# Two copies on GpSimd that feed batch 3's transpose, placed on two sides of a hold

## The chip, the cores and the metric

The kernel runs on one core of one Trainium2 chip. A core has five engines with queues of their own: TensorE (PE in the profile; PEld are its weight loads), VectorE (DVE), ScalarE (ACT), GpSimd (POOL) and SyncE (SP), which here only issues transfers. An engine works through its own queue in order and waits on semaphores for the others. The metric is the time of one execution on the device, in microseconds; the median of ten runs of the kernel before is 205.81.

## The reference

For each of 8 batches and 8 heads, with x (512 x 64) and state (32 x 64):

```python
scores = scale * np.matmul(x, state.transpose(0, 1, 3, 2))
a = softmax(scores);   xread = np.matmul(a, state)
a2 = softmax(scale * np.matmul(state, x.transpose(0, 1, 3, 2)))
sread = np.matmul(a2, x)
attn = np.concatenate([xread, sread], axis=2)       # 512 + 32 rows a batch
h = attn_as_rows @ w_in                             # (4352 x 512) @ (512 x 2048)
out = (0.5 * h * (1 + erf(h / sqrt(2)))) @ w_out    # (2048 x 512)
```

(`softmax` stands for the shifted exponentials over their sum that the reference spells out, and `attn_as_rows` for its transpose and reshape.)

## The kernel before, in words

**Work of one batch.** The 512 rows of a batch lie as 128 partitions by SJ = 4 groups. The steps are:

- `load_x(b)` brings x of one batch into `xb` as bf16, by a transfer issued from GpSimd's queue (512 KB).
- `rearr(b)` makes two GpSimd copies, one for each half t of the heads, from `xb` into `x4`, in the order that the transpose wants (L224, 128x1024 each). There are two tiles `x4`, used by even and odd batches in turn.
- `xtr_dma(b)` issues a transposing transfer from `x4` to `xT` on SyncE's queue (L277). It reads all of `x4`, so it needs both copies.
- `scores(b, half)` multiplies `xT` with the state (L330), and ScalarE takes the exponentials into `e` (L337).
- `norm(b, half)` is three VectorE instructions: sums (L350), reciprocals (L352) and the scaling of `e` into `a` (L353). "Batch 2's scaling" is L353 of batch 2, twice, for two halves.
- `atr_dma(b)` issues a transposing transfer from `a` to `AT`, on SyncE (L373).
- `p_mm` makes P, the product of state and w_in, on TensorE (L421); copies on ScalarE and VectorE empty its banks (L432, L433; for batch 2's first half L1094 and L1096).
- `mm1` (called `M`) multiplies P with `AT` (L484), and ScalarE takes the GELU into `g` (L491). M(16b) to M(16b+15) are batch b's.
- The second matrix product goes from `g` to the output. For batch 0 it is plain (`mm2`, `mm2_m`, called `U`); for the others it is Strassen's form with seven products, `X(b, "1")` to `X(b, "7")` (L581), whose sums of `g` (`g_sum`, L575) and of w_out (`w_sums`, L547) are made on VectorE, and a few sums on GpSimd (L600, L636).
- `sread`, `srt` and the later `SR` and `R` make the 32 extra rows of each batch; `rearr_ones(b)` makes the copy `xo` of x that `sread` needs (L234, GpSimd for b of 2 and more).

**Order.** Nothing plans the order: the schedule is manual, and each engine runs its instructions in the order in which the program calls them. The calls are written out by hand up to line 1103 and by a loop over batches 2 to 7, with eight slots p each, after that. Batch b + 1's attention is prepared between batch b's products: in the loop, `scores(3, ...)` stand at b = 2, p = 1, behind M(32, 33), pmat(2, 2) and X(1, "4").

**Banks.** The PSUM pool `ps_f` has four buffers in turn, used by `mm1`, `scores`, some `p_mm` tiles, `state_prep`, `sread` and `srt`; the pool `ps_o` has four banks o0 to o3, one buffer each.

**Holds.** `hold` is one column that GpSimd copies from a tile that is to be waited for. It puts a wait into GpSimd's queue: what stands behind it starts after that tile is written. `hold_for(b, m)` (L902) waits for a slice of `g`; line 1079 waits for `a` of batch 2, that is for both halves of batch 2's scaling.

The lines around the change:

```python
    norm(2, 0)
    norm(2, 1)
    atr_dma(2)
    nc.gpsimd.tensor_copy(out=hold, in_=atts[2].a[:, 0, 64:65])
    begin(3)
    rearr(3)
    xtr_dma(3)
```

`begin(3)` only names batch 3's tiles and takes `xT`'s buffer; it gives no instruction. GpSimd's queue before the hold ends with load_x(3) and load_st(3, B), called some lines earlier.

Of the kernel before, what the change touches and what calls it, by code (L numbers as in the profile page):

```python
# [17 lines left out]
def kernel(  # L18
# [136 lines left out]
    def state_prep(b0, b1, pool=ps_f, tag="f"):  # L155
        n = b1 - b0
        ps = pool.tile([128, n, HC, NS], BF16, name="st_ps", tag=tag)
        for b in range(b0, b1):
            nc.tensor.transpose(
                ps[:, b - b0, :, :].rearrange("p c n -> p (c n)"),  # L160
                st_bf[:, b, :, :].rearrange("q t d -> q (t d)"),
                ident,
            )
        for t in range(2):
            nc.vector.tensor_copy(
                out=sbd[64 * t:64 * t + 64, b0:b1, :, 32 * t:32 * t + 32].rearrange(
                    "d b c n -> d (b c) n"
                ),
                in_=ps[64 * t:64 * t + 64, :, :, :].rearrange("d b c n -> d (b c) n"),
            )  # L170
# [34 lines left out]
    def begin(b):  # L205
        A = Att()
        atts[b] = A
        A.x4 = x4s[b % 2]
        A.xo = xos[b % 2]
        if b > 0:  # L210
            A.xT = att.tile([128, SJ, HC, 128], BF16, name="xT", tag="xT")
# [5 lines left out]

    def rearr(b):  # L220
        A = atts[b]
        src = xbs[b].rearrange("p (t c) (j d) -> p t c j d", t=2, d=D)
        for t in range(2):
            nc.gpsimd.tensor_copy(  # L224
                out=A.x4[:, :, :, 64 * t:64 * t + 64].rearrange("p j c d -> p c j d"),
                in_=src[:, t],
            )
# [47 lines left out]
    def xtr_dma(b):  # L275
        A = atts[b]
        nc.sync.dma_start_transpose(  # L277
            out=A.xT.rearrange("p j c n -> p (j c) n"),
            in_=A.x4.rearrange("p j c n -> p (j c n)"),
        )  # L280
# [198 lines left out]
    def mm1(b, m):  # L479
        if m == 0:  # L480
            gs[b] = gpool.tile([128, MC, S], BF16, name="g", tag="g")
        hp = ps_f.tile([128, S], FP32, name="hp", tag="f")
        for t in range(2):
            nc.tensor.matmul(  # L484
                hp,
                lhsT=Ps[b][:, t, m * 128:(m + 1) * 128],
                rhs=atts[b].AT[:, :, t, :],
                start=(t == 0),
                stop=(t == 1),
            )  # L490
        nc.scalar.activation(out=gs[b][:, m, :], in_=hp, func=AF.Gelu)  # L491
# [48 lines left out]
    def w_add(name, x, y, op):  # L540
        if name == "3":
            pair = persist.tile([128, 2, MH, NH], BF16, name="ws_34", tag="mix0")
            w_sum["3"], w_sum["4"] = pair[:, 0], pair[:, 1]
        elif name != "4":
            tag = {"6": "mix1", "1": "mix2", "7": "mix3"}[name]
            w_sum[name] = persist.tile([128, MH, NH], BF16, name=f"ws_{name}", tag=tag)
        nc.vector.tensor_tensor(out=w_sum[name], in0=x, in1=y, op=op)  # L547

    def w_sums(i):
        (b11, b12), (b21, b22) = w_q  # L550
        w_add(*(
            ("3", b12, b22, ALU.subtract),
            ("4", b21, b11, ALU.subtract),
            ("6", b11, b12, ALU.add),
            ("1", b11, b22, ALU.add),
            ("7", b21, b22, ALU.add),
        )[i])
# [347 lines left out]
    def M(*ms):  # L905
        for m in ms:
            mm1(m // MC, m % MC)
# [147 lines left out]
    w_sums(0)  # L1055
    begin(2)
    rearr(2)
    xtr_dma(2)
    hold_for(0, 15)
# [4 lines left out]
    U(13)  # L1064
    state_prep(2, 3, ps_o, "o3")
    w_sums(1)
    M(18, 19)
    M(20, 21)
    U(14)
# [7 lines left out]
    norm(2, 1)  # L1077
    atr_dma(2)
    nc.gpsimd.tensor_copy(out=hold, in_=atts[2].a[:, 0, 64:65])
    begin(3)  # L1080
    rearr(3)
    xtr_dma(3)
    M(24, 25)
    M(26, 27)
# [20 lines left out]
    for b in range(2, B):  # L1105
        nb = b + 1
        for p in range(8):
# [40 lines left out]
            if p == 0 and nb + 1 < B:  # L1148
                begin(nb + 1)
                rearr(nb + 1)  # L1150
# [36 lines left out]
    b = B - 1  # L1187
# [40 lines left out]
```

## Time and profile before

| what | value |
| --- | --- |
| median of 10 runs | 205.81 us (205.42 to 207.54) |
| profiled execution | 206.21 us |
| its span | 204.4 us |
| TensorE busy | 197.4 us (97%) |
| VectorE busy | 156.9 us (77%) |
| ScalarE busy | 135.3 us (66%) |
| GpSimd busy | 69.8 us (34%) |
| granted TensorE clock | 1.0 throughout |
| L224, 12 copies on GpSimd | 13.6 us, mean 1162 ns |
| L234, 12 copies on GpSimd | 15.7 us, mean 1340 ns |
| L353, 14 scalings on VectorE | 10.4 us, mean 742 ns |

The profile is of one execution. Its span runs from the first instruction of the program to the end of the last; the execution's time is 1.8 us longer. A line of the timeline gives start and length in us, engine, line of the kernel, operation, tiles (written <- read), shapes, how many instructions were joined, and in brackets how long the engine stood idle before it and what ended that. In the chain, each row is the work, wait or transfer that the end of the kernel hung on at that time. All times inside the span are in us from its start.

### The profile page before, as it was taken

What the parts mean: (1) busy time and instruction counts of PE and PEld (TensorE: products, weight loads), DVE (VectorE), ACT (ScalarE), POOL (GpSimd) and SP (SyncE); (2) the same over time, 40 slices, a digit from 0 to 9 for tenths busy, and PEclk for the clock granted to TensorE, in tenths of its full rate; (3) what the DMA queues carried; (4) which work ended last, traced back from release to release, by engine and by line L of the source; (5) the groups of instructions that cost most, each with busy time, mean ns of one, the idle gap of its engine ahead of it and who ended that gap; (6) DMA issues with size and microseconds to landing.
All of it is one profiled execution on the core that took longest, in us unless ns stands there. A gap on an engine that the chain in (4) does not pass through costs nothing.

```text
span 204.4 us, 4911 instructions
## 1 busy us (share of the span) xinstructions
PE 197.4 (97%) x2039; PEld 133.4 (65%) x2039; DVE 156.9 (77%) x254; ACT 135.3 (66%) x240; POOL 69.8 (34%) x77
## 2 busy tenths in 40 slices
PE   7799999999799999999999999999999999999994
PEld 2443544465476667766875777667776787878893
DVE  2853777879888888977897787678778988895883
ACT  3685677689596669675966788587847666864120
POOL 8893303306544558271625702340220002200000
PEclk9999999999999999999999999999999999999999
DMA  6999997994866688736483504660106001040125
GB/s 196 186 179 200 205 199 119 136 256 88 125 90 147 201 108 100 163 138 70 59 174 102 133 0 102 71 196 0 51 3 205 3 0 55 0 157 0 51 100 162
DMA packets 40566, 23.16 MB, mean 113 GB/s; under 512 B 21856, under 2 KB 39136, under 8 KB 40544
## 3 DMA queue, kind: packets, MB, share of 16 engines
q0 software_dynamic: 13984, 8.10, 29.6%
q1 hardware_dynamic: 25872, 14.36, 27.9%
q10 hardware_dynamic: 688, 0.39, 0.6%
q8 instruction: 16, 0.26, 0.5%
q14 instruction: 6, 0.05, 0.1%
HBM read 17.30 MB, written 8.91 MB: 128 GB/s over the span
## 4 chain that ended last, share of the span: by engine, by line
PE 87%; DMA 6%; DVE 2%; ACT 2%; POOL 1%; issue 0%; SPq 0%; POOLq 0%
PE xp L581 38%; PE hp L484 24%; PE op L526 5%; PE p_ps L421 4%; PE sp L788 3%; PE rp L854 3%; DMA xT<-x 3%; DMA x0f<-in_x_dram 3%; PE xp L693 2%; PE pt L330 1%; PE sr L384 1%; PE op L510 1%; PE hp L1005 1%; POOL x L224 1%; DVE a L353 1%; PE warm_ps L149 1%
## 5 line engine op out<-in xcount | busy, mean ns | idle before, releaser
L491 ACT ACTIVATE g<-hp 128x512 bf16<-128x512 f32 x124 | 67.1, 605 | 26.5 <-PE hp L484 19.9
L484 PE MATMUL hp<-AT,P 128*128 128x512 bf16 x248 | 63.1, 379 | 0.1
L581 PEld LDWEIGHTS <-gsum 128*128 128x128 bf16 x528 | 51.0, 98 | 12.1 <-issue 2.1
L575 DVE TENSOR_TENSOR gsum<-g 128x2048 bf16<-128x2048 bf16 x35 | 45.7, 1321 | 0.9 <-ACT g L491 0.9
L484 PEld LDWEIGHTS <-P 128*128 128x128 bf16 x248 | 22.8, 98 | 20.7 <-issue 2.9
L581 PE MATMUL xp<-ws,gsum 128*128 128x256 bf16 x304 | 36.3, 273 | 0.0
L581 PE MATMUL xp<-ws,g 128*128 128x256 bf16 x224 | 26.7, 273 | 0.0
L581 PE MATMUL xp<-w_out_bf,gsum 128*128 128x256 bf16 x224 | 26.6, 273 | 0.0
L581 PEld LDWEIGHTS <-g 128*128 128x128 bf16 x224 | 21.8, 98 | 4.8 <-issue 0.2
L433 DVE CAST P<-p_ps 128x512 bf16<-128x512 f32 x29 | 18.8, 684 | 3.5 <-PE p_ps L421 3.4
L636 POOL TENSOR_TENSOR u<-s,oh 128x512 f32<-128x512 f32 x6 | 7.8, 1304 | 39.5 <-ACT oh L633 39.5
L432 ACT CAST P<-p_ps 128x512 bf16<-128x512 f32 x29 | 15.8, 599 | 6.1 <-PE p_ps L421 5.8
L224 POOL COPY x<-xb 128x1024 bf16<-128x1024 bf16 x12 | 13.6, 1162 | 14.7 <-DMA xb<-in_x_dram 14.7
L234 POOL COPY xo<-xb 128x1024 bf16<-128x1024 bf16 x12 | 15.7, 1340 | 4.3 <-PE sr L384 4.3
L600 POOL TENSOR_TENSOR v<-q,oh 128x512 f32<-128x512 f32 x6 | 8.3, 1390 | 23.5 <-ACT oh L638 20.8
L526 PE MATMUL op<-w_out_bf,g 128*128 128x512 bf16 x48 | 11.8, 380 | 0.0
L353 DVE TENSOR_TENSOR a<-e,ics 128x512 bf16<-128x512 bf16 x14 | 10.4, 742 | 0.5
L421 PE MATMUL p_ps<-w_in_bf,sbd 64*32 64x512 bf16 x248 | 10.4, 382 | 0.0
L350 DVE TENSOR_REDUCE cs<-e 128x16 f32<-128x512 bf16 x14 | 9.5, 677 | 0.6 <-ACT e L337 0.5
L411 DVE COPY XSR<-srT 128x128 bf16<-128x128 bf16 x8 | 5.7, 759 | 5.4 <-PE srT L408 5.4
L337 ACT ACT_TABLE_LOAD x7 | 9.0, 1283 | 0.1
L491 ACT ACT_TABLE_LOAD x7 | 9.0, 1283 | 0.1
(129 smaller groups left out, 227.6 us busy)
## 6 DMA issues: line engine op xcount, KB each, us to landing
out_dram<-oh SPq DMA_DIRECT2D x15, 256.0 KB, 2.4
xb<-in_x_dram POOLq DMA_DIRECT2D x7, 512.0 KB, 6.8
out_dram<-oh SPq DMA_DIRECT2D x6, 512.0 KB, 2.8
w_in_bf<-in_moe_w_in_dram POOLq DMA_DIRECT2D x6, 256.0 KB, 9.8
out_dram<-osb SPq DMA_DIRECT2D x5, 256.0 KB, 5.8
w_out_bf<-in_moe_w_out_dram POOLq DMA_DIRECT2D x4, 256.0 KB, 6.9
w_out_bf<-in_moe_w_out_dram POOLq DMA_DIRECT2D x2, 512.0 KB, 12.4
x0f<-in_x_dram SPq DMA_DIRECT2D x3, 256.0 KB, 3.9
```

The costliest lines, as they stand in the source:

```text
L224: nc.gpsimd.tensor_copy(out=A.x4[:, :, :, 64 * t:64 * t + 64].rearrange("p j c d -> p c j d"), in_=src[:, t],)
L234: eng.tensor_copy(out=A.xo[:, :, :, 2 + 64 * t:66 + 64 * t].rearrange("p j c d -> p c j d"), in_=src[:, t],)
L350: nc.vector.reduce_sum(out=cs, in_=e4, axis=AX.X)
L353: nc.vector.tensor_tensor(out=A.a[:, :, hs].rearrange("p g (c n) -> p g c n", n=NS), in0=e4, in1=ics[:, :, :].to_broadcast((128, G, 2, NS) ...
L421: nc.tensor.matmul(ps[t][32 * c:32 * c + 32, :], lhsT=sbd[64 * t:64 * t + 64, b, c, 32 * t:32 * t + 32], rhs=w_in_bf[64 * t:64 * t + 64, c ...
L432: nc.scalar.copy(out=dst[:, 0, :], in_=ps[0])
L433: nc.vector.tensor_copy(out=dst[:, 1, :], in_=ps[1])
L484: nc.tensor.matmul(hp, lhsT=Ps[b][:, t, m * 128:(m + 1) * 128], rhs=atts[b].AT[:, :, t, :], start=(t == 0), stop=(t == 1),)
L491: nc.scalar.activation(out=gs[b][:, m, :], in_=hp, func=AF.Gelu)
L526: nc.tensor.matmul(ops[b, j], lhsT=gs[b][:, m, j * 128:(j + 1) * 128], rhs=w_out_bf[:, m, :], start=(m == 0), stop=(m == MC - 1),)
L575: nc.vector.tensor_tensor(out=t, in0=g_q(b, h0, k0), in1=g_q(b, h1, k1), op=op)
L581: nc.tensor.matmul(ps[:, j - js[0], :], lhsT=lhs[:, m, 128 * j:128 * j + 128], rhs=rhs[:, m, :], start=(first and j == js[0] and m == 0), ...
```

## The change

`rearr` gets a second argument, the halves t that it copies. The call for batch 3 is parted in two. The copy of half 0 is called earlier, behind `state_prep(2, 3, ...)` and `w_sums(1)`; on GpSimd's queue that is right behind load_st(3, B) and ahead of the hold, so it waits for x of batch 3 alone. The copy of half 1 stays behind the hold. The transposing transfer is called at the same place as before. The queues of TensorE, VectorE, ScalarE and SyncE have the same instructions in the same order as before; on GpSimd's queue one copy and the hold have changed places.

```diff
-    def rearr(b):
+    def rearr(b, ts=(0, 1)):
         A = atts[b]
         src = xbs[b].rearrange("p (t c) (j d) -> p t c j d", t=2, d=D)
-        for t in range(2):
+        for t in ts:
             nc.gpsimd.tensor_copy(
                 out=A.x4[:, :, :, 64 * t:64 * t + 64].rearrange("p j c d -> p c j d"),
                 in_=src[:, t],
...
     state_prep(2, 3, ps_o, "o3")
     w_sums(1)
+    begin(3)
+    rearr(3, (0,))
     M(18, 19)
...
     nc.gpsimd.tensor_copy(out=hold, in_=atts[2].a[:, 0, 64:65])
-    begin(3)
-    rearr(3)
+    rearr(3, (1,))
     xtr_dma(3)
```

## The prediction

> **What bounds the kernel now.** I read the page first, then the chain that ended last in order of time, then TensorE's gaps, then the four engines and the transfers around the one gap that the change can touch.
>
> The page says that TensorE sets the time, and that its clock is never cut:
>
> ```profile
> PE 197.4 (97%) x2039; PEld 133.4 (65%) x2039; DVE 156.9 (77%) x254; ACT 135.3 (66%) x240; POOL 69.8 (34%) x77
> PEclk9999999999999999999999999999999999999999
> ```
>
> The chain in order of time is TensorE almost from 12 us on, with one large detour, which runs through the lines of the change:
>
> ```profile
> 46.76 0.27 DVE ics L352
> 47.05 0.70 DVE a L353
> 47.80 0.08 issue
> 47.88 0.19 POOL hold L1079
> 48.06 0.74 POOL x L224
> 48.81 0.17 issue
> 48.98 1.04 POOL x L224
> 50.04 5.78 DMA xT<-x
> 55.82 0.05 issue
> 55.87 0.64 PE pt L330 x16
> ```
>
> Batch 2's scaling (L353) releases the hold, GpSimd makes its two copies one after the other, SyncE starts the transposing transfer, and TensorE waits for its landing before batch 3's scores. TensorE's timeline gives the size of that wait; behind it no gap above 0.06 us comes until the end, so what is taken from it reaches the end of the kernel unless something new waits:
>
> ```profile
> 55.87 0.64 PE L330 MATMUL pt<-sbd,xT 128*128 128x64 bf16 x16 [1.36 <-DMA xT<-x]
> ```
>
> So at most 1.36 us can be gained: TensorE ended X(1,"4") at 54.50.
>
> **The first copy, moved.** x(3) was issued at 36.45 and landed 10.1 us later, at 46.58 (query of the tile xb in that window). GpSimd stands idle from 38.27, so the copy starts at about 46.63 (batch 4's started 0.05 us after its landing) and takes 1.04 (L224's usual duration): to 47.67. No instruction and no transfer is added; one copy of 1.04 us goes from behind the hold to before it. What then stands behind the copy's wait for x on GpSimd's queue is the hold, the second copy, the hold on batch 1's g, the two copies into xo, the hold on batch 2's g and load_x(4); all of them stood behind the later hold before, so none loses.
>
> **What the copy meets on VectorE.** From 46.63 to 47.67 VectorE does the sums (46.05 to 46.73), the reciprocal (to 47.01), and from 47.05 the scaling, which reads e and ics, both in SBUF. Batch 3's scaling shows the same meeting:
>
> ```profile
> 59.08 1.04 POOL L224 COPY x<-xb 128x1024 bf16<-128x1024 bf16 x1 [4.80 <-DMA xb<-in_x_dram]
> 59.62 1.03 DVE L353 TENSOR_TENSOR a<-e,ics 128x512 bf16<-128x512 bf16 x1
> ```
>
> There it took 1.03 instead of 0.69 and ended 0.54 after GpSimd's copy; at 83.18 and 104.46 it ended 0.55 after the GpSimd instruction that it met. So here it ends at 47.67 + 0.54 = 48.21 instead of 47.74: 0.47 late. The Trainium skill, "SBUF — State Buffer", section "Who interferes with whom", speaks against the change more strongly: a VectorE instruction with two SBUF inputs contends with a GpSimd instruction that reads SBUF, and the one that comes second is fully blocked. Fully blocked, it would run its whole 0.69 after 47.67, to 48.36: 0.62 late. By the rule the gain below is 0.75 us, by the rows 0.90. I take the rows, since three agree.
>
> **What is late next.** Behind the scaling on VectorE come three casts (L1094) that empty p_ps. The weight loads and VectorE's first cast, by their timelines:
>
> ```profile
> 47.66 0.68 DVE L1094 CAST P<-p_ps 128x512 bf16<-128x512 f32 x1
> 48.40 0.53 PEld L484 LDWEIGHTS <-P 128*128 128x128 bf16 x3 [0.26 <-issue]
> ```
>
> The cast ends at 48.34 and the weights of M(30) load at 48.40: M(30) takes the bank that this cast empties, and waits for it now already. So 0.47 on the scaling is 0.47 on M(30) and on all of TensorE up to the scores: X(1,"4") ends at 54.97 instead of 54.50. That is the price, and it is paid before the wait, where it only shortens it. The rest is covered: the second cast frees X(1,"6")'s bank at 49.41, against 50.01; x(3)'s neighbour AT(2) is issued at 48.28 and with its 3.1 lands at 51.37, against M(32)'s start at 51.75; the state copies (L165) end near 51.2, needed at 52.7. ScalarE runs with TensorE; its table load for the exponentials ends at 55.31, before the first scores at 55.38.
>
> **The second copy and the transfer.** The hold runs 0.14 after the scaling (48.35), the copy starts 0.11 after the hold (48.46) and ends at 49.50; before it ended at 50.02. SyncE must first issue AT(2), which occupies it for 1.25 from 48.28, to 49.53. So xT(3) is issued at 49.53 instead of 50.04: 0.51 earlier, not the 1.04 of the copy.
>
> Its 5.78 to landing is the longest of six (4.3 to 5.8, median 4.7). The windows of the transfers say why: 51.00 to 53.75 moves at full rate, then 1.25 us almost nothing, and in that stretch lies one packet of another queue:
>
> ```profile
> 51.00:53.75 2.75, 2.75 (x28) 1.72 (x26) 2.20 (x3) 1.95 (x5) 2.58 (x4) 1.00 1.06 193
> 53.75:55.00 1.25, 0.75 (x7) 0.43 (x5) 1.21 (x2) 1.09 (x1) 0.52 (x1) 1.00 0.07 8
> q8 instruction: 1, 0.02, 2.4%
> ```
>
> (the first columns are time and length, the last two DMA share and GB/s). All but one DMA engine were done at 53.8; one was held about 0.95 us by a 16 KB instruction fetch at 53.42, and then shared with x(4)'s first packets. After the change the transfer's data lies about 0.5 earlier, from near 50.7 (AT(2)'s must go first) to 53.4; the fetch comes with TensorE's progress, so near 53.9. Without the collision it lands at 49.53 + 4.26 (batch 4's) + 0.25 for AT(2)'s tail = 54.0; with the full 5.78 at 55.31. I take the first, since the cause of the long one has moved apart; even a landing at 54.9 would cost nothing, as TensorE comes at 54.97.
>
> **The sum.** Scores start at 54.97 instead of 55.87: 0.90 us. Of the 1.36 us of stall all goes, and 0.47 comes back as VectorE's delay. With the long transfer it is 55.87 - 55.36 = 0.51. The profiled execution took 206.21 (span 204.4 and 1.8 around it), so it becomes 205.3. The median of the runs is 205.81, 0.40 below the profiled one; nothing shown says where those 0.40 lie. If they are a shorter stall (as the transfer's spread allows), the gain is 0.50 and the median 205.3; if they lie elsewhere, 0.90 and 204.9. I take the middle: 205.05.
>
> **Behind the scores.** VectorE is 0.47 late while TensorE is 0.90 early, and it works without a break from 53.36 to 60.65. It reaches batch 3's scaling at 60.09 instead of 59.62, there meets both copies of x(4) instead of one (59.05 to 61.07) and ends at 61.6 instead of 60.65. It then had 1.11 of idle time before q (L642) and 0.70 before L608; both take up most of it. The next TensorE step that waits for VectorE is the p_ps of P(3), at 68.77, which needs L644 (ended 68.12): it now comes at 67.87, and I have L644 at about 67.6. The margin shrinks from 0.65 to 0.3, and I count nothing.
>
> **Rivals.**
> *Gain cut (0.2 to 0.5 us; 205.3 to 205.6).* x(3) lands 0.4 later than in this trace, so the scaling comes first and blocks the copy, as the second copy at 60.05 was (it ended 0.91 after the scaling): then 48.65, the second copy about 49.8, the transfer 0.25 earlier, in front of the same fetch. Or the fetch still holds it. For: one landing time only is known. Against: 0.4 is much for a load issued 10 us ahead.
> *No move (205.8).* x(3) lands after the scaling, over 1.1 us later than traced; then the hold costs nothing now, and the order of the two is no matter.
> *Slower (206.7): the debt on VectorE.* Place: L644 before P(3)'s p_ps. Price: a 128x2048 sum of g that meets GpSimd took up to 2.60 (at 99.81) against the 1.51 of the sum at 62.37 that stands here, 1.09 more; and the scaling of batch 3's second half, late enough to meet v (L600), would lose about what the first half does, 0.95. It decides when L644 ends after 68.72: then TensorE starts P(3) later than the 68.77 of now. I have it at 67.6; with both it is 69.65, and TensorE starts 0.93 later than before, 206.7, as nothing behind gives that back. For: VectorE has no idle time from 53 to 61, and the change moves GpSimd's work against it. Against: the idle 0.70 before L608, and u and v on GpSimd follow TensorE. One of the two alone ends near 205.8 or 205.9.
> *More than counted (204.5).* The scaling isn't held at all and the whole 1.36 goes.
>
> **How the numbers follow.** 0.3% is 0.62 us, about what can be told from no change. Stall gone, debt paid: 0.55 (204.8 to 205.4; three quarters of it beyond 0.62). Gain cut: 0.22. No move: 0.06. Slower: 0.12, a little of it within 0.3%. More: 0.05. So faster 0.42 + 0.05 = 0.47; within 0.13 + 0.22 + 0.06 + 0.02 = 0.43; slower 0.10. The range from 204.5 to 206.1 leaves out most of the slower case and the lower half of the best, under 2 in 10; the likeliest case alone is 204.8 to 205.4.
>
> **What would show it.** In the changed profile: one L224 copy at about 46.6 and one at 48.5; L353 of batch 2 at 1.1 to 1.2 instead of 0.69; M(30)'s weights at about 48.9; xT(3) issued at 49.5, landed before 55; no gap, or under 0.1, before L330 at about 55.0. It is wrong if x(3) lands after 47; if the gap before L330 stays with a landing of over 5 us; or if TensorE shows a new gap behind VectorE between 58 and 70, or anywhere after.

## The result, and the profile after

The changed kernel takes 204.66 us (median of 14 runs, 204.03 to 205.75), beside 205.98 for the kernel before in the same comparison. The ratio is 0.9932, 95% interval 0.991 to 0.9953, or 1.4 us less; the two medians are 1.3 us apart. A ratio, here and below, leaves out executions that took over 1.5% more than the fastest of their kernel. The profiled execution took 205.59 us, with a span of 203.8.

In the timeline of TensorE in the changed kernel (start and length in us, what it does, in brackets its idle time before), the wait ahead of batch 3's scores is gone:

```profile
54.72 0.71 PE L581 MATMUL xp<-ws,g 128*128 128x256 bf16 x5
55.26 0.63 PE L330 MATMUL pt<-sbd,xT 128*128 128x64 bf16 x16
```

The second line is the one that bore 1.36 us of idle time before; it bears none. The execution is only 0.6 us shorter in span than the one before because it has a wait of its own, 12 us earlier, at batch 2's scores:

```profile
42.87 0.64 PE L330 MATMUL pt<-sbd,xT 128*128 128x64 bf16 x16 [0.98 <-DMA xT<-x]
```

That is batch 2's transposing transfer, issued at 34.35 and landed after 8.5 us, against 4.8 in the profile before. Nothing ahead of it was changed, and two further profiles of the changed kernel (below) show 0.27 and none. TensorE waited there in three of the eight profiles of the changed kernel and its variants (the one with x asked for earlier left aside), and in none of the four with both copies behind the hold; whether that is chance isn't shown. From the start of batch 2's scores to that of batch 3's is 14.23 us before (41.64 to 55.87) and 12.39 after (42.87 to 55.26). That stretch holds everything that the change touches up to the scores, and I use it below to compare profiles, since it leaves out what happens earlier.

GpSimd's and VectorE's timelines of the same execution, around the copies:

```profile
47.06 1.04 POOL L224 COPY x<-xb 128x1024 bf16<-128x1024 bf16 x1 [8.71 <-DMA xb<-in_x_dram]
48.80 0.19 POOL L1081 COPY hold<-a 128x1 bf16<-128x1 bf16 x1 [0.69 <-DVE a L353]
48.92 1.04 POOL L224 COPY x<-xb 128x1024 bf16<-128x1024 bf16 x1
...
47.69 0.25 DVE L352 RECIPROCAL ics<-cs 128x16 f32<-128x16 f32 x1
47.98 0.69 DVE L353 TENSOR_TENSOR a<-e,ics 128x512 bf16<-128x512 bf16 x1
```

The copies are parted as written. But the second scaling took 0.69, not the 1.1 to 1.2 forecast: TensorE's wait at 42.87 had made VectorE late, x had landed 0.96 ahead of the scaling, and the copy was nearly done when it began (it ended at 48.10, 0.12 after the scaling's start). So either this execution was lucky, or the forecast debt isn't ordinary.

### The profile page after: what moved, and what is told of

It is laid out like the page before. It is cut to its first block, busy times and chain, and to the rows that moved or that the text cites. A ratio compares the mean times of both kernels' runs of the same rounds, so it can differ in the third digit from the quotient of the medians.

```text
span 203.8 us, 4911 instructions
## 1 busy us (share of the span) xinstructions
PE 197.6 (97%) x2039; PEld 133.5 (65%) x2039; DVE 156.9 (77%) x254; ACT 135.3 (66%) x240; POOL 68.9 (34%) x77
## 4 chain that ended last, share of the span: by engine, by line
PE 80%; DMA 15%; POOL 1%; DVE 1%; issue 0%; ACT 0%
PE xp L581 41%; PE hp L484 22%; DMA w_out_bf<-in_moe_w_out_dram 11%; DMA xT<-x 4%; PE p_ps L421 3%; PE sp L788 3%; PE rp L854 3%; PE xp L693 2%; PE warm_ps L149 2%; PE pt L330 1%; PE sr L384 1%; PE xT_ps L256 1%; POOL a L315 1%; PE op L510 0%; DVE xT L260 0%; POOL xb L117 0%
## 5 line engine op out<-in xcount | busy, mean ns | idle before, releaser
L636 POOL TENSOR_TENSOR u<-s,oh 128x512 f32<-128x512 f32 x6 | 8.8, 1466 | 40.8 <-ACT oh L633 40.8
L224 POOL COPY x<-xb 128x1024 bf16<-128x1024 bf16 x12 | 12.6, 1079 | 23.5 <-DMA xb<-in_x_dram 23.5
L234 POOL COPY xo<-xb 128x1024 bf16<-128x1024 bf16 x12 | 14.7, 1257 | 4.4 <-PE sr L384 4.4
L421 PE MATMUL p_ps<-w_in_bf,sbd 64*32 64x512 bf16 x248 | 10.3, 382 | 0.0
```

The source lines that it names most:

```text
L224: nc.gpsimd.tensor_copy(out=A.x4[:, :, :, 64 * t:64 * t + 64].rearrange("p j c d -> p c j d"), in_=src[:, t],)
L234: eng.tensor_copy(out=A.xo[:, :, :, 2 + 64 * t:66 + 64 * t].rearrange("p j c d -> p c j d"), in_=src[:, t],)
L421: nc.tensor.matmul(ps[t][32 * c:32 * c + 32, :], lhsT=sbd[64 * t:64 * t + 64, b, c, 32 * t:32 * t + 32], rhs=w_in_bf[64 * t:64 * t + 64, c ...
```

## The experiments

Theory: the gain is the early issue of batch 3's transposing transfer, which clears TensorE's instruction fetch and then lands before TensorE comes; the early copy costs what it takes from batch 2's scaling. Rivals: the meeting is never paid for; the gain comes from emptier queues and not from the transfer; the wait before was an accident of one execution.

**Both kernels again.** No edit.

> The changed kernel once more. The recorded theory (the first copy meets batch 2's second scaling, which loses about 0.47 us and passes it to M(30); the wait before batch 3's scores goes): L353 of batch 2's second half 1.1 to 1.2 us, TensorE at batch 3's scores 0.4 to 0.5 later than it would be without the copy, no gap there, about 0.9 us faster than before. Rival, that the copy and the scaling miss each other and nothing is paid (as in the profile of the changed kernel at hand, in which batch 2's scores had waited 0.99 us for a late transfer, so that VectorE came late): L353 at 0.69 and 1.2 to 1.4 us faster.

> The changed kernel once more, for its profile: where x lands between batch 2's two scalings, and what the second one loses. If the recorded 0.47 is ordinary, its L353 takes 1.0 to 1.2 and M(30) waits 0.4 to 0.6; if not, 0.69 and at most 0.15. In both no gap before batch 3's scores.

> The kernel before once more, for its profile. If the wait of 1.36 us at batch 3's scores is its ordinary state, there is one of 0.9 to 1.4 again, with a fetch near the transfer's end and a landing of over 5.3 us. If it was an accident of that execution, the wait is 0.1 to 0.4 and the landing 4.3 to 4.8.

The changed kernel: 204.66 us (22 runs) against 205.75, ratio 0.9939 (0.9919 to 0.9958). In its two profiles the second scaling takes 0.69 again. The third profile shows why, VectorE first, then GpSimd and SyncE:

```profile
44.33 0.69 DVE L353 TENSOR_TENSOR a<-e,ics 128x512 bf16<-128x512 bf16 x1
...
45.94 0.69 DVE L353 TENSOR_TENSOR a<-e,ics 128x512 bf16<-128x512 bf16 x1
...
44.56 1.36 POOL L224 COPY x<-xb 128x1024 bf16<-128x1024 bf16 x1 [7.23 <-DMA xb<-in_x_dram]
...
46.70 1.25 SPq L373 DMA_TRANSPOSE AT<-a  x1
48.03 1.95 SPq L277 DMA_TRANSPOSE xT<-x  x1
```

x landed at 44.51. The copy met the first scaling, which had already begun; so it was the copy that waited (1.36 instead of 1.04), and it was over at 45.92, just before the second scaling. TensorE's timeline has no wait of more than 0.1 us from 40 to 72. The stretch from scores to scores is 12.70.

The kernel before, in its second profile:

```profile
55.22 0.64 PE L330 MATMUL pt<-sbd,xT 128*128 128x64 bf16 x16 [1.23 <-DMA xT<-x]
```

Issue to landing was 5.65, the stretch 14.09. So the wait is no accident of one execution. This one took 205.55 us, 0.66 less than the first, with only 0.13 less of wait: what lay between the first profile and the median wasn't the stall. Most of it lies at the start: TensorE begins batch 1's scores at 21.74 in the first profile and at 21.23 in this one. But x landed at 44.55 here, 1.99 us ahead of the second scaling, where the first profile had 0.47.

**The meeting forced.** The first copy behind a hold on the sums of batch 2's second half, so that it starts right before the scaling:

```diff
         nc.vector.reduce_sum(out=cs, in_=e4, axis=AX.X)
+        A.cs = cs
...
-    begin(3)
-    rearr(3, (0,))
     M(18, 19)
...
     atr_dma(2)
+    begin(3)
+    nc.gpsimd.tensor_copy(out=hold, in_=atts[2].cs[:, 0, 0:1])
+    rearr(3, (0,))
     nc.gpsimd.tensor_copy(out=hold, in_=atts[2].a[:, 0, 64:65])
     rearr(3, (1,))
```

> The changed kernel with one more hold ahead of the first copy, on the sums of batch 2's second half, so that the copy starts just before the second scaling and always meets it. Recorded theory: the copy runs from about 0.25 after the sums' end to 1.3 after it, the scaling ends 0.54 behind it, 0.8 us late; M(30) and all of TensorE up to batch 3's scores are late by as much; the wait at the scores is gone. Against the kernel before: 1.36 minus 0.8, about 0.5 us faster; against the changed kernel 0.35 slower if that one pays 0.47, 0.8 slower if it pays nothing. Rival, that a late scaling is taken up before the scores: as fast as the changed kernel.

VectorE, GpSimd and TensorE of that run:

```profile
46.36 1.53 DVE L354 TENSOR_TENSOR a<-e,ics 128x512 bf16<-128x512 bf16 x1
...
46.30 1.04 POOL L224 COPY x<-xb 128x1024 bf16<-128x1024 bf16 x1
...
48.54 1.02 PE L485 MATMUL hp<-AT,P 128*128 128x512 bf16 x4 [0.81 <-DVE P L1097]
```

The copy ends at 47.34 and the scaling at 47.89, 0.55 behind it and 0.84 late. M(30) waits 0.81 for the cast behind the scaling, and the stretch is 13.53, that is 0.83 above the 12.70. So the debt exists, and goes to TensorE one to one. In time it is 205.06 us, ratio 0.9964 (0.9947 to 0.9981), 0.40 over the changed kernel on the same chip (the intervals of the two ratios overlap), half of the 0.8 that was to be expected if that one paid nothing. So ordinary executions of the changed kernel may lose something of their own. Its profiles show waits of 0.98 and 0.27 at batch 2's scores and no debt; how it divides in the others stays open.

**The transfer late again.** The changed kernel with its second copy made twice:

```diff
     rearr(3, (1,))
+    rearr(3, (1,))
     xtr_dma(3)
```

> The changed kernel with the second copy made twice, so that the transposing transfer is issued 1.0 us later, about where the kernel before issues it, while the first copy stays early. If the gain comes from the transfer's start ahead of TensorE's fetch and of TensorE's arrival, the wait at batch 3's scores is back (1.0 to 1.4 us, landing over 5.3) and the time is that of before, 205.7. If the gain comes from the emptier GpSimd and VectorE around the hold, it stays near the changed kernel, 204.7 to 205.0.

```profile
45.91 0.69 DVE L353 TENSOR_TENSOR a<-e,ics 128x512 bf16<-128x512 bf16 x1
...
49.03 1.81 SPq L277 DMA_TRANSPOSE xT<-x  x1
...
54.51 0.64 PE L330 MATMUL pt<-sbd,xT 128*128 128x64 bf16 x16 [1.15 <-DMA xT<-x]
```

206.15 us, ratio 1.002 (1.0001 to 1.004). The first copy is as early as in the changed kernel, and only the issue is late: 2.43 us after the end of the second scaling, where the changed kernel has 1.40 and the one before 2.30. The wait is back (landing 5.43 after issue), and the whole gain is gone. The time is even a little above that of before; part of that is in the profile, where TensorE takes 22.17 us from batch 3's scores to batch 4's instead of 21.79. So the early first copy alone gains nothing: the issue has to be early. But the doubled copy also keeps GpSimd 1.1 us longer, so this run doesn't part the issue from an emptier GpSimd. The scores called later, below, do: there GpSimd's queue is as before.

**The fetch moved.** In both kernels the matmuls on the tile `warm` at the start are cut into pieces of 64 columns, which makes 109 more matmuls and shifts where TensorE's fetches fall:

```diff
-            w = 128 * min(n, 4)
             nc.tensor.matmul(
-                ps[:, 0:w], lhsT=warm[:, 0:128], rhs=warm[:, 0:w], start=True, stop=True
+                ps[:, 0:64], lhsT=warm[:, 0:128], rhs=warm[:, 0:64], start=True, stop=True
             )
-            n -= 4
+            n -= 0.5
```

> The kernel before with the matmuls that keep TensorE warm at the start cut into pieces of 64 columns: 109 more matmuls of the same total width, which only shift where in the program TensorE's 16 KB instruction fetches fall; the copies and the hold stand as before. If the long landing (5.78) of batch 3's transposing transfer is due to the fetch at 53.4 on one DMA engine, it lands 4.3 to 4.8 us after its issue now, the wait before the scores falls from 1.36 to 0.1 to 0.4, and the time falls by about 1 us. If the fetch has no part in it, the wait stays at 1.3 and the time is that of before.

> The changed kernel with the same cut of the warming matmuls as the last experiment, so that no instruction fetch of TensorE falls into batch 3's transposing transfer. If the change gains by taking the transfer out of the fetch's way, then with the fetch gone on both sides there is no wait at the scores to save, and the parted copies are as fast as the unparted ones under the same cut (205.4) or slower by what the scaling loses (up to 0.5). If it gains by GpSimd's queue being done earlier as well (batch 4's load issued earlier, so that its copies meet less of VectorE's work and the 0.6 us that TensorE lost at 67 to 70 in that run go), it is up to 0.6 faster, 204.8.

The transfers of the kernel before in the window 50.7 to 55.2 of its second profile, and then of the same copies with the fetch moved, 50.7 to 53.9 (DMA share in 40 slices; the queue's kind, packets, MB, share):

```profile
DMA  5999999999999999999900000000000699999727
q8 instruction: 1, 0.02, 1.3%
```

```profile
DMA  3899999999999999999999999999999420000000
q1 hardware_dynamic: 2080, 0.52, 87.8%
xT<-x SPq DMA_TRANSPOSE x1, 4.3
```

With a fetch in the window the DMA engines stop at about 53, one is left over for more than a microsecond, and the last packets come with batch 4's load. Without it the transfer runs through and lands after 4.26. The fetches next to it now begin at 43.73 and 56.74. TensorE then starts batch 3's scores without a wait, with GpSimd's copies still both behind the hold:

```profile
53.85 0.64 PE L329 MATMUL pt<-sbd,xT 128*128 128x64 bf16 x16
```

The stretch is 12.71, that of the changed kernel. So the long landing was the fetch's doing, as the prediction had it.

In time the kernel before with the fetch moved is 205.44, ratio 0.9973 (0.9952 to 0.9993): a third of a microsecond, not the one expected. Its profile is of a quick execution (204.77), so it can't hold all that is missing, but it shows one loss, 10 us behind the scores:

```profile
62.71 1.76 DVE L352 TENSOR_TENSOR a<-e,ics 128x512 bf16<-128x512 bf16 x1
```

Batch 3's second scaling was blocked for 1.07 by u on GpSimd (62.66 to 63.92), which was late because the copies of batch 4's x had themselves been blocked (3.26 us for the two). VectorE reached batch 3's banks late, and from batch 3's scores to batch 4's TensorE took 22.40 us instead of 21.79. The parted copies under the same cut have 12.70 and 21.78, and 204.72 us, ratio 0.9951 (0.9926 to 0.9977). By one profile of each, TensorE is 0.62 us faster there with the parted copies even with no fetch in the way. (That execution took 206.02 all the same: from batch 7's scores to the end it needed 1.9 us more than the other.) GpSimd comes earlier to batch 4's load with them (its hold ends, and the load is issued, 1.13 us ahead of batch 3's scores instead of 0.94), which I take for the cause; the intervals of the two ratios overlap, so by the clock it isn't settled.

**Both copies early.**

```diff
-    rearr(3, (0,))
+    rearr(3)
...
-    rearr(3, (1,))
```

> Both copies right when x of batch 3 lands, none behind the hold. Recorded theory: the first copy as in the changed kernel, the scaling slips in behind it or waits for both (1.0 to 2.1 us instead of 0.69), M(30) late by 0.5 to 1.4; SyncE issues the transposing transfer of x right behind that of a, as the copies are done by then, so there is no wait at the scores. Between 0.9 faster (one copy met) and 0.1 faster (both met) than before. Rival, that only the transfer's start matters: as fast as the changed kernel or faster.

204.94 us, ratio 0.9954 (0.9935 to 0.9974). In its profile x landed later than the second scaling began (47.22 against 47.06):

```profile
47.27 2.37 POOL L224 COPY x<-xb 128x1024 bf16<-128x1024 bf16 x2 [8.98 <-DMA xb<-in_x_dram]
...
55.63 0.64 PE L330 MATMUL pt<-sbd,xT 128*128 128x64 bf16 x16 [1.12 <-DMA xT<-x]
```

The copies were hardly early then: the transfer was issued 1.92 us after the second scaling, against 2.30 before, and the wait is there (5.92 from issue to landing). That is close to the "no move" of the prediction, seen in one execution of a relative of the change. In the median the two versions can't be told apart.

**The scores later.** Batch 3's scores behind M(34, 35), with the copies as before, and with the copies parted:

```diff
-            if p == 1 and nb < B:
+            if p == 1 and nb < B and b > 2:
                 scores(nb, 0)
...
             M(k, k + 1)
+            if b == 2 and p == 1:
+                scores(nb, 0)
+                scores(nb, 1)
```

> The kernel before with batch 3's scores called one pair of products later (behind M(34, 35)), the copies as before. TensorE has 0.86 us of work to do while the transfer comes in. If the wait at the scores is all that stands between the two kernels, it falls from 1.2 to 1.4 to 0.35 to 0.5, and the time by about 0.85, to 204.9. If what TensorE gains there is lost to VectorE's debt at 67 to 70, as it was with the fetch moved, the gain is 0.2 to 0.4 only.

> Both: parted copies and batch 3's scores one pair of products later. In the changed kernel there is no wait at the scores in three profiles, so the later call has nothing to hide: 204.6, as the changed kernel, or up to 0.2 faster if ordinary executions sometimes wait there.

With the copies as before, 204.93 us, ratio 0.996 (0.9935 to 0.9984):

```profile
55.28 0.64 PE L330 MATMUL pt<-sbd,xT 128*128 128x64 bf16 x16 [0.39 <-DMA xT<-x]
```

A pair of products of 0.86 us put in front takes 0.84 to 0.97 off the wait, and the median is 0.90 below the 205.83 of before. GpSimd has the same queue as before here, so the wait alone is worth most of the gain, whatever GpSimd does. With both: 205.16, ratio 0.9959 (0.9939 to 0.9979), not better than the changed kernel. Its profile has the debt in its ordinary form:

```profile
44.88 1.41 DVE L353 TENSOR_TENSOR a<-e,ics 128x512 bf16<-128x512 bf16 x1
...
44.71 1.04 POOL L224 COPY x<-xb 128x1024 bf16<-128x1024 bf16 x1 [6.76 <-DMA xb<-in_x_dram]
...
48.55 1.02 PE L484 MATMUL hp<-AT,P 128*128 128x512 bf16 x4 [0.66 <-DVE P L1095]
```

Here the copy began 0.17 before the first scaling, which lost 0.72, and M(30) waited 0.66. In the third profile of the changed kernel the scaling had begun 0.23 before the copy, and nothing was lost.

**x earlier.** So that the copy is over before it can meet anything:

```diff
-    hold_for(0, 15)
+    hold_for(0, 13)
     load_x(3)
```

> The changed kernel with batch 3's x asked for one pair of products earlier (the hold on batch 0's g waits for its slice 13, not 15), about 1.0 us. x lands near 45.5 instead of 46.6 in the time of the profile before, so the first copy is over before the second scaling starts. If an ordinary execution of the changed kernel pays for the meeting of copy and scaling, this one is 0.2 to 0.5 us faster than it (204.2 to 204.4). If it pays nothing, it is as fast as the changed kernel; if the earlier load lies across batch 2's transposing transfer, TensorE waits up to 1 us at batch 2's scores and it is slower.

```profile
44.25 0.93 PE L330 MATMUL pt<-sbd,xT 128*128 128x64 bf16 x16 [3.45 <-DMA xT<-x]
```

The median is 207.49 us (14 runs, 203.95 to 210.05) against 205.72: 1.8 slower. The ratio, 0.9986 (0.9943 to 1.0028), rests on five of the fourteen. The load now lies across batch 2's transposing transfer, which lands 10.3 us after its issue, and TensorE waits 3.45 us at batch 2's scores in this profile, of an execution of 208.68. So the danger that was named beforehand came true, larger than the 1 us expected. What the early landing would be worth can't be read from it. No version tried beats the changed kernel.

## Why the prediction was right, and where it was off

The direction and the range held; the gain was 1.4 us (1.25 by the ratio of the second comparison) where 0.76 was forecast. The main step, the earlier issue, was right, and the debt set against it did not come. By its steps:

- *What bounds the kernel: right.* The wait at batch 3's scores was the one thing to gain; it goes with the transfer's issue and comes back with it (1.15 in the run with the late copy).
- *The first copy's time: the step that failed.* "Landed 10.1 us later, at 46.58" was one execution's landing, taken as the rule. x lands 0.47 and 1.99 us ahead of the second scaling in the two profiles of the kernel before, and 0.96, 1.55 and 1.43 ahead in the three of the changed one; with both copies early it landed 0.16 behind the scaling's start. So "0.4 is much", said against the rival of a cut gain, was wrong: the landing spreads over 2 us.
- *What the copy meets: mechanism right, size off.* 0.47 was forecast on the second scaling; it was 0 in all three profiles. Forced, it is 0.84, with the scaling ending 0.55 behind the copy, as the rows of before had it. The Trainium skill's "SBUF — State Buffer" ("Who interferes with whom") would have the scaling run its whole 0.69 after the copy; three rows of before and the forced run agree on 0.54 to 0.55, so the measurement stands. That page's word that the one which starts first blocks the other is borne out by the two cases on the first scaling: 0.72 lost when the copy was 0.17 ahead, 0 when it was 0.23 behind.
- *What is late next: right as a path.* Where there is a debt, it goes over the cast to M(30), 0.84 to 0.81 and 0.72 to 0.66.
- *The transfer: right in cause, short in size, narrow in margin.* It is issued right behind that of a, as forecast. With no debt that is 1.40 us after the scaling instead of 2.30: 0.90 earlier, not 0.51. It landed after 4.55 to 4.69, near the 4.5 that I counted, against 5.65 and 5.78. But transfer and fetch did not move 0.5 apart: in all three profiles the fetch begins within 0.01 us of the end of the transfer's last packet, at 53.89 in the first. Why it stands right behind it isn't shown.
- *The sum.* Wait saved 1.36 or 1.23, debt 0 instead of 0.47: the stretch shrinks from 14.09 and 14.23 to 12.39, 12.40 and 12.70. (The first two begin after a wait at batch 2's scores; without one on either side it is 14.09 and 14.23 against 12.70.) What I had called "more than counted", with 1 chance in 20, is what the profiles show. And splitting the 0.40 between the profiled execution and the median was wrong: the second profile of the kernel before had all but the same wait at 205.55 us.
- *Behind the scores: the outcome right, the reason untested,* since VectorE's debt did not arise. From batch 3's scores to batch 4's TensorE takes 21.78 or 21.79 before and after. But the rival's debt at that place is real: 0.61 us with the fetch moved and 0.38 (22.17) with the doubled copy.

## What to carry to other kernels

A wait for a transfer can be worth more than the delay in its issue: here 0.9 us of issue decided over 1.2 to 1.4 us of waiting, since an instruction fetch lay near the transfer's end. Look at what stands between the last full slice of a transfer and its landing before you count the gain. And where a copy is moved to "when its data land", its neighbours are decided by the spread of that landing; take a second profile before you count a collision as certain, in either direction.

## What the runs showed of the hardware

A 16 KB instruction fetch of TensorE is one packet. Where it met batch 3's transposing transfer it took 0.88 to 0.97 us (elsewhere up to 1.7), and the transfer, where the fetch fell into its data, landed 5.4 to 5.8 us after its issue; with none, 4.3. The fetch can also meet the very end. Where it begins within 0.03 us of the transfer's last packet of data, batch 3's transfer landed 4.5 to 4.7 us after its issue in six profiles, but 5.9 in one, with batch 4's load behind it; batch 2's, with batch 3's load behind it, landed after 4.8, 6.1, 8.5 and 10.3.

The packets tell the 5.9 from the six. A transfer ends with packets of 4 bytes behind its data. In the six, the last of these came before the fetch. In the one (both copies early), the data ended at 53.57, the fetch ran from there to 54.50, and the last two packets of 4 bytes stand at 54.49 and 54.50, with nothing else of the transfer between:

```profile
q1 hardware_dynamic: 2, 0.00, 0.2%
```

(the transfer's queue in the window 53.6 to 54.8 of that run). The landing came 1.09 us after that, when batch 4's load had begun; in the two runs with the fetch moved it came 0.47 and 0.48 us after the last of them. That these packets are the completion mark, and that the load held up the rest, is what I infer; no run takes it apart.

A VectorE scaling (128x512, 0.69 us alone) that met a GpSimd copy lost up to 0.84 us when the copy had started first, and nothing when it had itself started first, by as little as 0.03 us; then the copy lost 0.3 to 0.5.
